# Six weight loads moved behind the first recurrence, and a mixed series of idle products, in a delta-rule attention and feed-forward kernel

## The chip, the cores and the metric

The kernel runs on one core of one Trainium2 chip. The metric is device time in microseconds; a lower time is better. The time before is the median of three runs. A core has five engines with instruction streams of their own: TensorE (PE; its weight loads, PEld, are instructions of their own), VectorE (DVE), ScalarE (ACT), GpSimd (POOL) and SyncE (SP), which here issues nearly all DMA transfers. They meet only at semaphores.

## The reference

Two parts in a row. First a delta rule: for each of 4 x 8 heads a 48 x 48 state is carried over 768 positions.

```python
for t in range(S):
    kt, vt, bt = (k_n[:, :, t], v[:, :, t], beta[:, :, t, None])
    y[:, :, t] = np.einsum('bhd,bhde->bhe', q[:, :, t], state)
    v_old = np.einsum('bhde,bhd->bhe', state, kt)
    state = state + bt[:, :, :, None] * np.einsum('bhd,bhe->bhde', kt, vt - v_old)
```

`k_n` is k over its norm. Then a feed-forward layer over the 3072 tokens, whose 384 columns are the heads' outputs side by side:

```python
h = x @ w_in
g = np.where(pos, h, np.where(neg, 0.0, (h + beta) ** 2 / (4.0 * beta)))
return (g @ w_out).astype(np.float32)
```

with beta = 1, `pos` where h >= 1 and `neg` where h <= -1, and 2048 hidden columns.

## The kernel before, in words

Positions are cut into 12 chunks of 64, and two chunks make a block (the code's G, 0 to 5). Within a chunk the recurrence becomes matrix products and the inverse of a 64 x 64 triangular matrix per head. The inverse is made by DVE for small diagonal blocks (`lanes`, `solve`, `unlanes`) and then put together by PE: `merge16_a` and `merge16_b` join 16-row blocks to 32, `merge32_a` and `merge32_b` join those to 64. `chain_r`, `chain_u`, `chain_y`, `chain_d` carry the state from chunk to chunk; `chain_y` leaves the outputs of a chunk as columns of `xb`, the feed-forward layer's input (part of them by six small DMAs on SP, L386).

The feed-forward layer has 16 weight tiles (`FT`), each with 128 hidden columns of w_in and w_out. They come packed, 768 KB each (`weight_loads`, L83), and are unpacked by a generator (`unpack`, `weight`) in steps on ACT and DVE (L125 to L137) into pairs of float32r parts, a large one and a remainder. `up` makes h (L524), `rest` and the lines around it the activation, `down` adds to the output (L539). A product takes three passes over the pairs of parts.

The order is written out by hand: each engine runs its instructions in the order in which the code issues them, and waits at semaphores.

- SP first issues, in this order, the inputs of chunks 0 and 1 (`load_w(0)`, `load_w(1)`), beta, weight tiles 0 and 1, `load_kv(0)`, `load_kv(1)`, and weight tiles 2 to 15. Transfers on this queue follow each other.
- PE first runs 14 warm-up products (L99), the Gram products of chunks 0 and 1 (`gram`, L146 and L147), and then `hold(KEEP, 512)`: 20 idle products of the zero tile SF, 128 x 128 by 128 x 512 (L473). They use no result and wait for none; DVE meanwhile solves the small blocks. The next work of PE is `merge16_a(0)`, which waits for DVE's transpose (L270).
- Then come the stages of chunk 0 and 1 (L482 to L499). Each `stage` issues PE's products, then steps of the unpacking (`wu`) and the scaling of v (`sv`) on ACT and DVE, then the reading out of the products. After `chain_y(0)` SP issues `load_w(2)`, the inputs of chunk 2 (L72 and L73), and after `chain_d(0)` `load_kv(2)`.
- From L502 on, items (block, weight tile) are run with `plan`, which places the next block's recurrence between them at fixed half items. For block 0 the Gram products of chunks 2 and 3 (L146 again) stand at items 2 and 4, `load_w(3)` at item 1.

PSUM banks for the products of the first part are handed out in rotation by `acc()` from the list START of eight; after `spare.clear()` (L500) the name `ch` with two banks is used. The name `ghi` with two buffers holds the large part of the activation.

In float32 one `nc.tensor.matmul` is two matmul instructions with a weight load each, four PE instructions; in float32r it is one matmul and one weight load.

Of the kernel before, what the change touches and what calls it, by code (L numbers as in the profile page):

```python
# [7 lines left out]
F32 = mybir.dt.float32  # L8
F32R = mybir.dt.float32r
# [4 lines left out]
C = 64  # L14
# [5 lines left out]
DF = 2048  # L20
FT = DF // 128
WARM = 14
KEEP = 20
PASSES = ((0, 0), (0, 1), (1, 0))
WHOLE = 2
LAG = 2
# [3 lines left out]
def delta_rule_moe(ctx: ExitStack, tc: tile.TileContext, kqa, kqb, kv, beta, w, out):  # L30
# [14 lines left out]
    nc = tc.nc  # L45
# [3 lines left out]
    NB = CB * C  # L49
    P = 128  # L50
# [4 lines left out]
    sb = ctx.enter_context(tc.tile_pool(name="sb", bufs=2))  # L55
    ps = ctx.enter_context(tc.tile_pool(name="ps", bufs=1, space=bass.MemoryType.PSUM))
# [6 lines left out]
    def acc():  # L63
        if spare:
            spare.append(spare.pop(0))
            return spare[-1]
        return dict(name="ch", bufs=2)

    def load_w(g, q=nc.sync):
        for i in range(NT):  # L70
            x = W[g, i] = sb.tile([P, 3, NV, C], F32, name="W", bufs=4)
            q.dma_start(out=x[0:C, 0:3:2], in_=kqb[g, i][:, 0:3:2])  # L72
            q.dma_start(out=x[C:C + D, 0:2], in_=kqa[g, i])  # L73

    def load_kv(g, q=nc.sync):
        for i in range(NT):
            KV[g, i] = sb.tile([P, 2, NV, D], F32, name="KV", bufs=4)
            q.dma_start(out=KV[g, i], in_=kv[g, i])

    def weight_loads(n0, n1):  # L80
        for f in range(n0, n1):
            RAW[f] = const.tile([P, 2, 2 * DM], F32, name=f"wt{f}")
            nc.sync.dma_start(out=RAW[f].bitcast(I32), in_=w.bitcast(I32)[:, f])  # L83
# [6 lines left out]
    weight_loads(0, 2)  # L90
    load_kv(0)
    load_kv(1)
    weight_loads(2, FT)

    warm = sb.tile([P, P], F32, name="wx")
    nc.vector.memset(warm, 0.0)
# [14 lines left out]
    SF = const.tile([P, 2 * NU * D + C - D], F32, name="SU")  # L111
# [299 lines left out]
    def finish(evicts):  # L411

        for p in [q() for q in evicts]:
            if p:
                p()

    def products(*pieces):
        return [p() for p in pieces]

    def both(f, g):  # L420
        return [lambda i=i: f(g, i) for i in range(NT)]

    def run(gen, n=99):
        for _ in range(n):
            if next(gen, 0) == 0:
                break
# [28 lines left out]
    def stage(pieces, *fill):  # L455
        evicts = products(*pieces)
        for gen, m in fill:
            run(gen, m)
        finish(evicts)
# [9 lines left out]
    idle = ps.tile([P, 512], F32, **acc())  # L469

    def hold(n, m):
        for _ in range(n):
            nc.tensor.matmul(idle[:, 0:m], SF[:, 0:P], SF[:, 0:m], start=True, stop=True)  # L473
    hold(KEEP, 512)
    run(ln, 2)
    for x in raws:
        x()
# [11 lines left out]
    stage(one_(merge32_b, 1), (sv[1], 2))  # L489
    stage(both(chain_u, 0), (wu, 3))  # L490
    stage(both(chain_y, 0), (wu, 3))
    load_w(2)
    stage(both(chain_d, 0), (wu, 1))
    load_kv(2)
# [21 lines left out]
    def cols(bs):  # L516
        return slice(bs[0] * NB, bs[-1] * NB + NB)
# [132 lines left out]
    for n, item in enumerate(items):  # L650
        H, c = 2 * n, cols(item[2])
# [79 lines left out]
```

## Time and profile before

| | us |
|---|---|
| median of 3 runs | 694.35 (694.16 to 696.31) |
| span of the profiled execution | 693.4 |
| PE busy | 637.4 |
| DVE busy | 437.2 |
| ACT busy | 397.7 |
| POOL busy | 44.8 |
| mean granted clock of PE | 0.956 |

Of the profiled execution the page gives the span, from the first to the last instruction, and no other time. Bytes read from HBM: 33.13 MB; written: 4.72 MB. Rows of the profile name the engine, the line of the kernel, the operation, the output and inputs by the program's names, the shapes and a count. The chain of waits follows the work that ended last back to the start; "issue" in it is time in which the engine waited for nothing that the profile shows. In tables of stretches a row has the busy time of each engine, the clock that was granted to PE as a share of full speed, the mean share of the DMA engines in use, and GB/s.

### The profile page before, as it was taken

Reading aid. Unit: us, or ns where it says so; the run is one execution under the profiler, and the core shown is the slowest. Engines: PE = TensorE matmul, PEld = TensorE weight load, DVE = VectorE, ACT = ScalarE, POOL = GpSimd, SP = SyncE. Lnnn points to the kernel's source line nnn. Section 1 sums busy time; section 2 is a strip of 40 time slices with the busy share of each in tenths; the row PEclk is TensorE's granted clock in tenths of the full one; section 3 lists DMA queues with packets and bytes.
Section 4 is the critical chain, followed back from the end, with each engine's and each line's share of the span. In section 5 each row is a group of like instructions: output and inputs, shape, how many; then the busy total and the mean of one; then the engine's idle time right before and its main releaser. Section 6 shows DMA issues by size and latency. Waiting matters only on the chain.

```text
span 693.4 us, 19365 instructions
## 1 busy us (share of the span) xinstructions
PE 637.4 (92%) x8428; PEld 552.6 (80%) x8428; DVE 437.2 (63%) x920; ACT 397.7 (57%) x720; POOL 44.8 (6%) x90
## 2 busy tenths in 40 slices
PE   9848876899999899999999999999999999999996
PEld 7338765678989788888888888788888788889895
DVE  3848788973455896446896447895457894433332
ACT  4227785556656556644457545557555468556663
POOL 3203042001000200000200000200000200000000
PEclk9956896799999999999999999999999999999999
DMA  8960430000161000043100153100242000001001
GB/s 244 418 267 9 120 103 1 0 3 4 24 171 53 24 1 2 18 109 98 46 2 2 41 122 81 28 1 2 60 123 79 9 1 3 14 12 46 0 1 46
DMA packets 18532, 41.45 MB, mean 60 GB/s; under 512 B 3600, under 2 KB 9104, under 8 KB 18448
## 3 DMA queue, kind: packets, MB, share of 16 engines
q1 hardware_dynamic: 18112, 40.04, 20.0%
q8 instruction: 66, 1.08, 0.7%
q14 instruction: 18, 0.15, 0.1%
q0 software_dynamic: 256, 0.08, 0.1%
q10 hardware_dynamic: 80, 0.10, 0.1%
HBM read 33.13 MB, written 4.72 MB: 55 GB/s over the span
## 4 chain that ended last, share of the span: by engine, by line
PE 54%; DVE 29%; ACT 6%; issue 5%; DMA 2%; SPq 2%; POOL 1%; DVEq 0%; POOLq 0%; ACTq 0%
PE o L539 17%; PE h L524 16%; DVE pr L247 5%; DVE A L249 4%; PE ch L146 4%; DVE glo L643 4%; PE ch L372 3%; DVE s L674 3%; PE ch L352 3%; PE ch L324 2%; PE ch L396 2%; DVE A L204 2%; PE ch L308 2%; DMA W<-in_kqa_dram 2%; PE ch L338 2%
## 5 line engine op out<-in xcount | busy, mean ns | idle before, releaser
L524 PE MATMUL h<-xb,wt 128*128 128x512 f32 (+1 forms) x936 | 230.6, 392 | 11.9 <-DVE s L674 10.6
L524 PEld LDWEIGHTS h<-xb,wt 128*128 128x128 f32 x936 | 166.5, 193 | 50.1 <-DVE s L674 15.8
L539 PE MATMUL o<-wt,ghi 128*128 128x384 f32 x768 | 201.7, 344 | 0.0
L539 PEld LDWEIGHTS o<-wt,ghi 128*128 128x128 f32 x768 | 138.9, 190 | 8.6 <-issue 1.5
L674 DVE TENSOR_TENSOR s<-h,s 128x512 f32<-128x512 f32 (+1 forms) x104 | 67.0, 644 | 112.9 <-ACT s L666 112.5
L539 PE MATMUL o<-wt,glo 128*128 128x384 f32 x384 | 130.9, 341 | 5.8 <-DVE glo L643 5.8
L642 ACT CAST ghi<-s 128x512 fp32r<-128x512 f32 (+1 forms) x104 | 61.3, 589 | 110.4 <-DVE s L674 81.4
L647 ACT ACTIVATE s<-h,half 128x512 f32<-128x512 f32 (+1 forms) x104 | 68.0, 654 | 55.8 <-PE h L524 55.1
L643 DVE TENSOR_TENSOR glo<-s,ghi 128x512 fp32r<-128x512 f32 (+1 forms) x104 | 67.1, 645 | 36.3 <-ACT ghi L642 35.9
L539 PEld LDWEIGHTS o<-wt,glo 128*128 128x128 f32 x384 | 72.8, 190 | 8.0 <-DVE glo L643 8.0
L647 ACT ACTIVATE s<-s,one 128x512 f32<-128x512 f32 (+1 forms) x104 | 71.8, 691 | 2.6
L666 ACT ACTIVATE s<-s 128x512 f32<-128x512 f32 (+1 forms) x104 | 62.3, 599 | 3.3
L146 PE MATMUL ch<-W 48*64 48x128 f32 x336 | 43.1, 278 | 9.3 <-ACT W L155 3.7
L146 PEld LDWEIGHTS ch<-W 48*64 48x64 f32 x336 | 37.2, 136 | 14.9 <-issue 5.5
L147 PE MATMUL ch<-W 48*64 48x128 f32 x336 | 43.4, 279 | 0.0
L247 DVE TENSOR_TENSOR pr<-A 128x30 f32<-128x30 f32 (+14 forms) x120 | 39.4, 328 | 5.5 <-POOL A L218 3.3
L249 DVE TENSOR_TENSOR A<-A,pr 128x30 f32<-128x30 f32 (+14 forms) x120 | 39.8, 332 | 4.4
L163 DVE TENSOR_TENSOR W<-ch,mask 64x256 f32<-64x256 f32 x64 | 27.0, 422 | 18.9 <-ACT GG L150 18.1
L150 ACT COPY GG<-ch 128x256 f32<-128x256 f32 x42 | 15.4, 374 | 38.5 <-PE ch L147 38.5
L147 PEld LDWEIGHTS ch<-W 48*64 48x64 f32 x336 | 37.2, 136 | 0.0
L218 POOL TENSOR_SCALAR_AFFINE_SELECT A<-A 128x1024 f32<-128x1024 f32 x4 | 5.1, 1265 | 365.4 <-DVE A L217 365.4
L407 DVE TENSOR_TENSOR SU<-ch,SU 48x384 f32<-48x384 f32 x40 | 22.2, 555 | 9.2 <-PE ch L396 8.5
(137 smaller groups left out, 705.6 us busy)
## 6 DMA issues: line engine op xcount, KB each, us to landing
wt<-in_w_dram SPq DMA_DIRECT2D x16, 768.0 KB, 13.7
KV<-in_kv_dram SPq DMA_DIRECT2D x24, 384.0 KB, 5.7
W<-in_kqb_dram SPq DMA_DIRECT2D x24, 256.0 KB, 4.7
W<-in_kqa_dram SPq DMA_DIRECT2D x24, 192.0 KB, 4.8
out_dram<-wx SPq DMA_DIRECT2D x47, 96.0 KB, 2.2
xb<-X SPq DMA_DIRECT2D x66, 32.0 KB, 2.0
xb<-A SPq DMA_DIRECT2D x6, 32.0 KB, 2.0
beta_sb<-in_beta_dram POOLq DMA_DIRECT2D x8, 10.0 KB, 2.4
```

What stands on the lines that cost most here:

```text
L146: nc.tensor.matmul(gp[0:C, p], w_[C:C + D, 0, u, :], w_[C:C + D, 0:2, u, :], start=True, stop=True)
L147: nc.tensor.matmul(gp[C:P, p], w_[0:D, 0, u, :], w_[0:D, 0:3:2, u, :], start=True, stop=True)
L163: nc.vector.tensor_tensor(out=w_[r:r + C, s, us[0]:us[0] + NP], in0=gp[r:r + C, :, 1, :], in1=mask[r:r + C, None, :].broadcast_to([C, NP, ...
L247: nc.vector.tensor_tensor(out=pr, in0=A[:, 0:n, j:j + 1].broadcast_to([P, n, m]), in1=A[:, j:j + 1, j + 1:32].broadcast_to([P, n, m]), op= ...
L249: nc.vector.tensor_tensor(out=A[:, 0:n, j + 1:32], in0=A[:, 0:n, j + 1:32], in1=pr, op=ALU.add)
L524: nc.tensor.matmul(h[:, cols(bs)], WT[f][:, 0, x, k * P:(k + 1) * P], XB[G][:, y, k, cols(bs)], start=(n == 0), stop=(n == 8))
L539: nc.tensor.matmul(oacc[G, k], (ghi, glo)[x][:, k * P:(k + 1) * P], WT[f][:, 1, y, :], start=(new and n == 0), stop=(left[G, b] == 0 and n ...
L642: nc.scalar.copy(out=ghi[:, c], in_=s[:, c])
L643: nc.vector.tensor_tensor(out=glo[:, c], in0=s[:, c], in1=ghi[:, c], op=ALU.subtract)
L647: nc.scalar.activation(out=out, in_=in_, func=AF.Relu, bias=bias, scale=scale)
L666: nc.scalar.activation(out=s[:, c], in_=s[:, c], func=AF.Square)
L674: nc.vector.tensor_tensor(out=s[:, c], in0=h[:, c], in1=s[:, c], op=ALU.max)
```

## The change

Weight tiles 2 to 9 stay where they were; the loads of tiles 10 to 15 are issued after the stage of `chain_y(0)`, before `load_w(2)`. The 20 idle products become 12 of the same form, then 32 and 16 products of zeros of 64 x 64 by 64 x 64 over the four quarters of the array in two orders, 6 products of a float32r tile of zeros (128 x 128 by 128 x 512), 32 products of 32 x 32 by 32 x 32 on four blocks of the array, and 4 of the first form. They write to `idle` and to a second PSUM bank, `other`, taken from the rotation. The zeros in float32r are written by POOL into a buffer of the name `ghi`.

```diff
-KEEP = 20
+KEEP = 12
+SOON = 10
...
-    weight_loads(2, FT)
+    weight_loads(2, SOON)
...
     hold(KEEP, 512)
+    other = ps.tile([P, 512], F32, **acc())
+    zr = sb.tile([P, 2 * NB], F32R, name="ghi", bufs=2)
+    nc.gpsimd.memset(zr.bitcast(F32), 0.0)
+
+    def quarters(n, w, order):
+        for j in range(n):
+            for r, c in order:
+                nc.tensor.matmul((idle, other)[r // C][c:c + w, j * w:j * w + w], SF[r:r + w, 0:w], SF[r:r + w, 0:w], start=True, stop=True)
+    quarters(8, C, ((0, 0), (C, C), (C, 0), (0, C)))
+    quarters(4, C, ((0, 0), (0, C), (C, 0), (C, C)))
+    for _ in range(6):
+        nc.tensor.matmul(idle, zr[:, 0:P], zr, start=True, stop=True)
+    for j in range(8):
+        for r, c in ((32, 0), (96, C), (0, 32), (C, 96)):
+            nc.tensor.matmul((idle, other)[r // C][c:c + 32, j * 32:j * 32 + 32], SF[r:r + 32, 0:32], SF[r:r + 32, 0:32], start=True, stop=True)
+    hold(4, 512)
     run(ln, 2)
...
     stage(both(chain_y, 0), (wu, 3))
+    weight_loads(SOON, FT)
     load_w(2)
```

## The prediction

> **What bounds the kernel now.** I read the page first, then the chain of waits, then the engine timelines of the first 100 us, where every edit lies.
>
> ```profile
> span 693.4 us, 19365 instructions
> PE 637.4 (92%) x8428; PEld 552.6 (80%) x8428; DVE 437.2 (63%) x920; ACT 397.7 (57%) x720; POOL 44.8 (6%) x90
> q8 instruction: 66, 1.08, 0.7%
> ```
>
> Over the span PE is the bound, but the edits lie in the first recurrence, between 34 and 65 us, and there it is another. The chain, in order of time (start, length, what):
>
> ```profile
> 32.09 2.19 DVE XT L270
> ...
> 36.42 4.21 issue
> ...
> 42.54 4.17 issue
> ...
> 48.60 1.83 issue
> ...
> 52.60 1.29 issue
> 53.88 2.82 PE o L308 x97
> ...
> 57.42 0.46 issue
> ```
>
> These five stretches of "issue" are 4.21 + 4.17 + 1.83 + 1.29 + 0.46 = 11.96 us in which PE waits for no engine and no tile. The PE timeline says what they are:
>
> ```profile
> 34.42 1.63 PE L281 MATMUL ch<-XT,GG 32*32 32x16 f32 x127 [2.76 <-DVE XT L270]
> 35.83 0.21 PE L281 MATMUL h<-XT,GG 32*32 32x16 f32 x1
> 35.87 0.21 PE L281 MATMUL ch<-XT,GG 32*32 32x16 f32 x1
> 35.87 0.55 PE L281 MATMUL h<-XT,GG 32*32 32x16 f32 x25
> 40.63 1.53 PE L281 MATMUL h<-XT,GG 32*32 32x16 f32 x100 [4.21 <-issue]
> 41.95 0.24 PE L293 MATMUL h<-A,XT 32*32 32x16 f32 x2
> 41.99 0.22 PE L281 MATMUL h<-XT,GG 32*32 32x16 f32 x2
> 42.01 0.53 PE L293 MATMUL h<-A,XT 32*32 32x16 f32 x24
> ```
>
> Between the first two stalls PE runs 100 + 2 + 2 + 24 = 128 matmuls, with their 128 weight loads 256 instructions. The queue q8 moved 66 packets, and PE's 2 x 8428 instructions over 66 are 255 each: q8 is PE's instruction fetch, and PE stops at the end of a block of 256 until the next has come. Before the first stall it ran 154 pairs, 308 instructions: 52 of one block and the whole next. So one block is fetched ahead, asked for when PE enters the block before. From entry to the next block's arrival: 40.63 to 46.70, **6.07 us**; then 46.70 to 50.43, 50.43 to 53.88, 53.88 to 57.89 (the ends of the stalls), mean **3.73 us**. What changes in between is the data transfers, in a table of stretches:
>
> ```profile
> 26.00:28.00 2.00, 2.00 (x6) 0.86 (x5) 1.79 (x7) 0.00 (x0) 0.00 (x0) 1.00 1.00 412
> 44.00:46.00 2.00, 0.00 (x0) 0.00 (x0) 0.00 (x0) 0.15 (x1) 0.00 (x0) 0.50 0.83 331
> 64.00:66.00 2.00, 2.00 (x50) 2.00 (x48) 0.68 (x2) 1.47 (x4) 0.00 (x0) 0.60 0.01 4
> ```
>
> (Columns: busy PE, PEld, DVE, ACT, POOL; granted clock, DMA share, GB/s.) The sixteen weight tiles fill the DMA engines until 0.83 of the way through 44 to 46, about 45.6 us. A fetch costs 6.07 us under them and 3.73 us without. A merge of 16-row blocks has 256 instructions, one block, and runs in 1.9 us (40.63 to 42.54): even a free DMA leaves this stage bound by the fetch.
>
> **The change, part by part.**
>
> *Six weight loads leave the front.* One is 768 KB, at 412 GB/s 1.91 us; six are 11.45 us, so the DMA engines come free at 45.6 - 11.45 = 34.1 us instead of 45.6.
>
> *The idle products.* One 128x512 product is two matmuls and two weight loads. Their time, and nearest rows for the other forms (the PE timeline and, for L352, L524 and L308, the chain):
>
> ```profile
> 14.22 17.43 PE L473 MATMUL ch<-SU 128*128 128x512 f32 x40
> 149.74 1.26 PE L281 MATMUL ch<-XT,GG 32*32 32x16 f32 x128 [0.21 <-DVE KV L343]
> 176.62 2.00 PE ch L352 x64
> 154.49 2.29 PE h L524 x9
> 167.40 1.13 PE ch L308 x64
> ```
>
> Twenty took 17.43 us (0.87 each). The new series: 12 big ones 10.46 us. Then 48 products on 64x64 quarters, 96 matmuls: the 64x64 matmuls of L352 go at 31 ns on two quarters, on all four between 31 and half of it, so 1.5 to 3.0 us. Six float32r products: L524 has that form, 0.254 us each, 1.5 us. Then 32 products of 32x32, 64 matmuls, between the 9.8 ns of L281 on four blocks and the 17.7 ns of L308 on two: 0.6 to 1.1 us. Four big ones 3.49 us. Sum 17.6 to 19.6 us; it ends between 31.8 and 33.8, before DVE has the transpose (34.28) on which the merge waits. I take 33.4. The PE gap before the merge shrinks from 2.76 us to about 1; a shorter gap alone gains nothing, because DVE sets the start.
>
> *Their instructions.* Before: 20 x 4 = 80. After: 48 + 128 + 64 + 12 + 128 + 16 = 396, 316 more. The merge began with 308 instructions in hand; 308 - 316 + 256 = **248** now, with the following block asked for 8 instructions, two big products, before the idle series ends: 33.4 - 1.7 = 31.7 us. That block's predecessor is asked for in the first quarters, near 26, and with 6.07 us arrives near 32, so I take 32.0: a stall inside the series of well under 1 us, which the 0.9 us before 34.28 cover.
>
> *The fetches, one after another.* Asked at 32.0, the first missing block comes between 32.0 + 3.73 = 35.7 and 32.0 + 6.07 = 38.1; the DMA engines come free in the middle, so I take 36.9. The following come every 3.73 us: 40.6, 44.4, 48.1, 51.8. They open instruction 248, 504, 760, 1016, 1272 of the stage; before, 308, 564, 820, 1076, 1332 opened at 40.63, 46.70, 50.43, 53.88, 57.89. The 60 instructions from 1272 to 1332 are 30 pairs of L308, 2.82 us for 97, 0.87 us: 52.7 against 57.89, **PE gains 5.2 us**. The second merge step of group 0 ends at instruction 768, just past 760, near 44.7.
>
> *What is late next.* DVE and ACT, which unpack the weights between the merges:
>
> ```profile
> 48.36 0.42 DVE L298 TENSOR_TENSOR XT<-XT,h 128x256 f32<-128x256 f32 x1 [8.54 <-PE h L293]
> ...
> 63.25 0.96 DVE L131 SCALAR_TENSOR_TENSOR xb<-wt,xb 128x768 int32<-128x768 int32 x1
> ...
> 66.35 0.96 DVE L137 TENSOR_TENSOR wt<-xb,wt 128x768 fp32r<-128x768 f32 x1 [1.67 <-ACT wt L135]
> ...
> 65.49 0.83 ACT L135 CAST wt<-xb 128x768 fp32r<-128x768 f32 x1
> ```
>
> From L298 at 48.36 DVE works with almost no gap until 64.68 (66.35 less its idle 1.67), so it gains what the second merge gains: 48.36 - 44.7 = 3.7 us. ACT's L135 at 65.49 needs L131, done at 64.21, 1.28 us earlier: it may gain 3.7 + 1.28 = 4.9. The smaller of 5.2 and 4.9 goes on: **-4.9 us** at the outputs of the first chunk.
>
> *The six loads in their new place* stand on SP's queue behind L386 and ahead of the second block's inputs, load_w(2) and load_kv(2); their 11.45 us of data go first.
>
> ```profile
> 2.00:4.00 2.00, 2.00 (x11) 2.00 (x11) 1.24 (x1) 0.30 (x2) 1.00 (x1) 1.00 0.85 210
> 73.39 1.40 SPq L72 DMA_DIRECT2D W<-in_kqb_dram  x1
> 74.83 0.59 SPq L73 DMA_DIRECT2D W<-in_kqa_dram  x1
> W<-in_kqa_dram SPq DMA_DIRECT2D x24, 192.0 KB, 4.8
> xb<-X SPq DMA_DIRECT2D x66, 32.0 KB, 2.0
> 87.12 0.29 PE L146 MATMUL ch<-W 48*64 48x128 f32 x1 [2.53 <-issue]
> 88.32 0.29 PE L146 MATMUL ch<-W 48*64 48x128 f32 x1
> 90.09 0.92 ACT L125 ACTIVATE xb<-wt 128x768 f32<-128x768 f32 x1
> 90.88 0.65 ACT L150 COPY GG<-ch 128x256 f32<-128x256 f32 x2
> ```
>
> All in the clock of before. The first tile starts moving near 73.4 + 1.8 (the small transfers land after 2.0), six end at 86.7, the first half of W(2), 448 KB at the 210 GB/s of such rows, at 88.8. The other bound: it landed at 74.83 + 4.8 = 79.6, plus 11.45 is 91.1. Its reader, the Gram product, began at 87.12; ACT takes the first result at 90.88, though it was done 1.2 us after the start: 2.6 us of cover. So 1.7 to 4.0 us late, less 2.6: 0 to 1.4 us, I take **+0.7**. Queued behind a waiting Gram product are PE's next products, behind a waiting L150 ACT's whole queue. Their own readers are no concern: tile 10 is first read by the eleventh L125, at 90.09. The issue of W(3), KV and the staging rows moves back as well, but their readers come later than W(2)'s by more than that.
>
> *At no cost:* the memset of the float32r operand and the second PSUM bank.
>
> ```profile
> 18.39 3.80 POOL L156 TENSOR_SCALAR_AFFINE_SELECT W<-W 64x256 f32<-64x256 f32 x8 [5.31 <-ACT W L155]
> ```
>
> POOL idles 5.31 us before its next work, and a memset of this size is half a us; without that gap it would delay L156 by as much. Every later bank of the rotation moves on by one, to banks emptied as long ago as before.
>
> **Sum.** 693.4 - 4.9 + 0.7 = 689.2 us of span. Of the profiled execution the page shows only the span, 0.95 us below the median of the runs, 694.35; so **690.2 us**.
>
> The Trainium skill, "Runtime: NRT & Kernel Launch", section "Instruction fetch mechanics", has blocks of 256 instructions as here, but says the fetch is hidden because issue is slower than the fill. By it the stalls would not be fetches and the time would stay near 694; the row above (256 instructions, then 4.17 us) speaks against it. It is the last rival below.
>
> **The rivals.**
>
> *More than I say (687.5).* If the first block comes by the free price, 35.7, and the rest at the best interval, 3.45: instruction 1332 at 35.7 + 4 x 3.45 + 0.87 = 50.4, 7.5 us gained on PE; the second merge at 42.9, 5.5 on DVE, 6.8 through ACT; nothing lost on W(2). For it: the queue is empty 2 us after the request. Against: the one fetch seen at the end of the transfers, asked for at 40.63, took the full 6.07.
>
> *The small products count as idle (692.9).* In the rows above the granted clock is 0.50 while 32x32 merges fill PE. If the quarters let it fall near 28 us, the rest of the series runs at half: it has reached 28 after 1.0 of the 1.5 us of float32r, the other 0.5 takes 1.0, the 32x32 products 1.7, the four big ones 7.0, end 37.7. The merge starts 3.3 us late but with its blocks in hand: instruction 248 at 39.6, the next ones at 43.3, 47.1, 50.8, 54.5, so 1332 at 55.4, 2.5 us gained on PE; the second merge at 47.4, 1.0 on DVE, 2.2 through ACT, less 0.7. Against: dense 64x64 products brought the clock back between 64 and 66 us.
>
> *Slower (699.4): the second block's inputs are starved.* The six tiles may move at the 210 GB/s of the mixed load instead of 412: 22.5 us, W(2) at 99.8, 12.7 us late less 2.6: +10.1 - 4.9. It outweighs the gain as soon as W(2) lands after 87.1 + 2.6 + 4.9 = 94.6. For it: rows of W are in that mix, and stand right behind the tiles. Against: tiles alone moved at 412 GB/s.
>
> *It doesn't do what it says (694.3).* The fetch is slow for another reason than the tiles, and stays at 6 us; the longer idle series then only moves the block borders.
>
> **How the numbers follow.** Forecast 0.56, more 0.17, counted as idle 0.11, starved 0.11, nothing 0.05. A measurement of this kernel tells 0.3%, 2.1 us, from no change: faster is below 692.3, slower above 696.4. Faster: 0.17, and 0.52 of the forecast's 0.56 and 0.02 from the idle case, 0.71. Slower: 0.11 and 0.01. Same: the rest, 0.17. The forecast's own range is 687.9 to 692.8 (the first block by its ends, W(2) by its own); the range of 8 in 10 takes in the first rival and the idle one: 686.3 to 695.0.
>
> **What would show it.** Right: "issue" before 60 us falls from 12 to about 6 us; the DMA share falls under 0.2 near 34; the first stall stands some 124 pairs into the merges and ends near 37; L298 starts near 44.7, L135 (now 65.49) near 60.6. Wrong: a stall still of 4 us at the second block; the merge starting after 34.6; a clock of 0.50 before 34; PE L146 of the second block waiting on DMA for more than 3 us.

## The result: 698.12 us, slower, and the profile after

The changed kernel takes 698.12 us (median of 18 runs, 695.31 to 702.79); the kernel before took 694.68 beside it (18 runs, 692.12 to 696.72). The ratio is 1.0052, 95% interval 1.0036 to 1.0069: slower by half a per cent. Forecast were 690.2 us, range 686.3 to 695.0. The profiled execution after took 697.55, with this on its page (span; PE's row; the queue of instruction fetches):

```profile
span 695.8 us, 19683 instructions
PE 637.3 (92%) x8586; PEld 554.8 (80%) x8586; DVE 437.6 (63%) x920; ACT 397.8 (57%) x720; POOL 45.3 (7%) x91
q8 instruction: 67, 1.10, 0.7%
```

PE's busy time is that of before (637.4): the 2.4 us are waiting. Lines of the changed kernel stand one further than before up to the idle products, and 17 or 18 further behind them: L281 is L282, L72 is L73, L146 is L147, L524 is L542.

**Up to 65 us the forecast came about.** The PE timeline after (start, length, line, operation, tiles, shapes, count, and in brackets the idle time before it with what ended it):

```profile
13.93 10.57 PE L474 MATMUL ch<-SU 128*128 128x512 f32 x24
24.42 1.63 PE L483 MATMUL ch<-SU 64*64 64x64 f32 x96
25.98 1.65 PE L487 MATMUL ch<-ghi 128*128 128x512 f32 x6
27.57 0.75 PE L490 MATMUL ch<-SU 32*32 32x32 f32 x64
...
30.81 1.88 PE L474 MATMUL ch<-SU 128*128 128x512 f32 x4 [0.58 <-issue]
34.15 1.22 PE L282 MATMUL h<-XT,GG 32*32 32x16 f32 x124 [1.46 <-DVE XT L271]
37.58 1.91 PE L282 MATMUL h<-XT,GG 32*32 32x16 f32 x128 [2.21 <-issue]
41.30 0.29 PE L282 MATMUL h<-XT,GG 32*32 32x16 f32 x4 [1.82 <-issue]
45.13 1.90 PE L294 MATMUL o<-A,XT 32*32 32x16 f32 x128 [1.85 <-issue]
48.86 0.24 PE L294 MATMUL o<-A,XT 32*32 32x16 f32 x3 [1.83 <-issue]
52.58 0.26 PE L309 MATMUL o<-XT,GG 32*32 32x32 f32 x2 [0.20 <-issue]
56.30 0.37 PE L325 MATMUL ch<-GG 32*32 32x32 f32 x5 [0.19 <-issue]
```

The series ends at 32.69 and the merge still starts when DVE lets it. The stalls of the merges sum to 2.21 + 1.82 + 1.85 + 1.83 + 0.20 + 0.19 = 8.10 us where five stretches of 11.96 stood. The table of stretches shows the DMA engines free just before 34:

```profile
32.00:34.00 2.00, 0.69 (x2) 0.00 (x0) 2.00 (x2) 0.00 (x0) 0.00 (x0) 1.00 0.82 336
34.00:36.00 2.00, 1.22 (x124) 1.15 (x124) 1.97 (x4) 0.00 (x0) 0.00 (x0) 1.00 0.11 42
```

The timelines of DVE and ACT after carry the gain on (the line set apart is the kernel before):

```profile
45.47 0.42 DVE L299 TENSOR_TENSOR XT<-XT,o 128x256 f32<-128x256 f32 x1 [5.92 <-PE o L294]
58.85 0.97 ACT L357 COPY SU<-h 64x384 f32<-64x384 f32 x2
61.29 0.83 ACT L136 CAST wt<-xb 128x768 fp32r<-128x768 f32 x1
```

```profile
63.04 0.97 ACT L356 COPY SU<-ch 64x384 f32<-64x384 f32 x2
```

The addition after the second merge is 48.36 - 45.47 = 2.9 us earlier, ACT's cast 65.49 - 61.29 = 4.2, and the first read-out of chunk 0 (L356 before, L357 after) 63.04 - 58.85 = 4.2.

**Behind 69 us it is lost.** The chain of waits after, which now runs through SP's queue (start, length, what):

```profile
69.12 1.34 SPq L84
...
72.72 0.46 SPq L84
...
73.98 15.49 DMA W<-in_kqa_dram
...
89.61 0.44 PE ch L147
```

The PE and ACT timelines at that place, and the stretches (three after, then one before):

```profile
78.85 1.32 PE L542 MATMUL h<-xb,wt 128*128 128x256 f32 x9
89.61 0.44 PE L147 MATMUL ch<-W 48*64 48x128 f32 x1 [9.43 <-DMA W<-in_kqa_dram]
...
91.62 0.37 ACT L151 COPY GG<-ch 128x256 f32<-128x256 f32 x1 [5.00 <-PE ch L148]
93.33 0.37 ACT L151 COPY GG<-ch 128x256 f32<-128x256 f32 x1 [1.33 <-PE ch L148]
```

```profile
80.00:84.00 4.00, 0.17 (x2) 0.00 (x0) 3.91 (x8) 1.95 (x4) 0.00 (x0) 1.00 1.02 375
84.00:88.00 4.00, 0.00 (x0) 0.00 (x0) 3.97 (x7) 1.57 (x3) 0.00 (x0) 0.57 1.06 200
88.00:92.00 4.00, 2.39 (x23) 2.42 (x25) 0.50 (x1) 0.37 (x1) 0.00 (x0) 0.50 0.71 201
```

```profile
88.00:94.00 6.00, 4.31 (x58) 3.61 (x54) 5.11 (x9) 4.46 (x12) 1.88 (x4) 1.00 0.97 252
```

PE stands still for 9.43 us because the first half of W(2) comes only at 89.47 (73.98 + 15.49). The Gram product of chunk 2, 4.2 us early until then, begins 2.5 us late (89.61 for 87.12), and at half the clock that it had before. The rest of the span keeps this: DVE's transpose of the next block's small matrices (L204, now L205) starts at 115.20, before at 113.36, and the span ends 2.4 us later.

### The profile page after: what moved, and what is told of

The parts are those of the page before. It is cut to its first block, busy times and chain, and to the rows that moved or that the text cites. A ratio compares the mean times of both kernels' runs of the same rounds, so it can differ in the third digit from the quotient of the medians.

```text
span 695.8 us, 19683 instructions
## 1 busy us (share of the span) xinstructions
PE 637.3 (92%) x8586; PEld 554.8 (80%) x8586; DVE 437.6 (63%) x920; ACT 397.8 (57%) x720; POOL 45.3 (7%) x91
## 4 chain that ended last, share of the span: by engine, by line
PE 56%; DVE 29%; ACT 5%; issue 4%; DMA 3%; SPq 1%; POOL 1%; DVEq 0%; POOLq 0%; ACTq 0%
PE o L557 18%; PE h L542 16%; PE ch L147 5%; DVE pr L248 5%; DVE A L250 4%; DVE glo L661 4%; DVE s L692 3%; PE ch L373 3%; PE ch L353 2%; DMA W<-in_kqa_dram 2%; PE ch L325 2%; PE ch L397 2%; PE ch L309 2%; DVE A L205 2%; PE ch L339 1%
## 5 line engine op out<-in xcount | busy, mean ns | idle before, releaser
L542 PE MATMUL h<-xb,wt 128*128 128x512 f32 (+1 forms) x936 | 228.9, 390 | 14.1 <-DVE s L692 12.6
L542 PEld LDWEIGHTS h<-xb,wt 128*128 128x128 f32 x936 | 165.3, 192 | 51.6 <-DVE s L692 17.7
L147 PE MATMUL ch<-W 48*64 48x128 f32 x336 | 43.2, 279 | 13.4 <-DMA W<-in_kqa_dram 9.4
L147 PEld LDWEIGHTS ch<-W 48*64 48x64 f32 x336 | 37.5, 137 | 18.8 <-issue 12.4
```

The costliest lines, as they stand in the source:

```text
L147: nc.tensor.matmul(gp[0:C, p], w_[C:C + D, 0, u, :], w_[C:C + D, 0:2, u, :], start=True, stop=True)
L542: nc.tensor.matmul(h[:, cols(bs)], WT[f][:, 0, x, k * P:(k + 1) * P], XB[G][:, y, k, cols(bs)], start=(n == 0), stop=(n == 8))
```

## The experiments

The theory (Q where a letter stands for it): the moved loads alone bring the gain in the first recurrence, by shorter fetches, and the same loads spend it again, because the second block's inputs stand behind them on SP's queue. Its rivals: the new series makes the difference, by the borders of the instruction blocks or by a cost of its own; or the gain is lost for a reason that has nothing to do with the order on the queue.

All ratios are against the kernel before, run beside on the same chip. "Read-out" is the first read-out of chunk 0, "Gram" the first Gram product of chunk 2, both from each kernel's one profiled execution; executions of one kernel differ by some 2 us, so the ratios decide.

| kernel | idle series | tiles 10 to 15 stand | ratio (95%) | read-out | Gram |
|---|---|---|---|---|---|
| before | 20 large | in front | 1 | 63.04 | 87.12 |
| after | new | ahead of W(2) | 1.0052 (1.0036 to 1.0069) | 58.85 | 89.61 |
| e1 | new | in front | 1.0025 (1.0009 to 1.0042) | 63.61 | 85.57 |
| e2 | 20 large | ahead of W(2) | 1.0014 (0.9998 to 1.0030) | 58.15 | 88.89 |
| e3 | new | behind KV(2) | 0.9978 (0.9963 to 0.9992) | 59.17 | 82.81 |
| e4 | 20 large | behind KV(2) | 0.9949 (0.9933 to 0.9964) | 58.07 | 82.32 |
| e5 | small ones first | behind KV(2) | 1.0056 (1.0029 to 1.0082) | 60.20 | 82.34 |
| e6 | new | 3 ahead of W(2), 3 behind KV(2) | 0.9976 (0.9957 to 0.9996) | 59.51 | 84.20 |
| e7 | small ones first | 2 behind KV(2), 4 behind KV(3) | 1.0011 (0.9996 to 1.0026) | 59.71 | 81.82 |
| e8 | 20 large | 2 behind KV(2), 4 behind KV(3) | **0.9898 (0.9879 to 0.9917)** | 57.38 | 79.65 |
| e9 | small ones first, 12 more | behind KV(2) | 0.9991 (0.9968 to 1.0015) | 59.12 | 83.06 |
| e10 | 20 large, 15 small | in front | 0.9974 (0.9959 to 0.9990) | 64.23 | 88.08 |
| e11 | 20 large, 15 small | behind KV(2) | 0.9954 (0.9934 to 0.9974) | 60.11 | 82.44 |
| e12 | new | 2 behind KV(2), 4 behind KV(3) | 0.9943 (0.9923 to 0.9962) | 59.57 | 83.29 |
| e13 | new without float32r | behind KV(2) | 0.9968 (0.9949 to 0.9987) | 57.72 | 79.66 |
| e14 | new without small products | behind KV(2) | 0.9942 (0.9923 to 0.9962) | 58.03 | 80.14 |
| e15 | 20 large, one in the second bank | behind KV(2) | 0.9929 (0.9912 to 0.9945) | 57.66 | 81.68 |

### One part of the change alone (e1, e2)

Only the new series, all sixteen tiles in front (against the changed kernel):

```diff
-    weight_loads(2, SOON)
+    weight_loads(2, FT)
...
-    weight_loads(SOON, FT)
```

> The new idle series alone; all sixteen weight tiles stay in front. Theory Q (the moved loads bring the gain and, standing ahead of W(2), the loss; the series does next to nothing): the fetches still cost about 6 us until the tiles have landed near 45.6, so the first read-out of chunk 0 (ACT L357, at 63.0 before and 58.9 in the changed kernel) comes at 61.5 to 63, no wait on the DMA of W(2), time 693 to 694.7. Rival S (the series brings the gain): L357 near 59 and a time near 690. Rival E (the loss comes from what the series changes, the bank rotation or the block borders): slower than before, 697 or more.

Only the loads, with the old series (against the kernel before):

```diff
-    weight_loads(2, FT)
+    weight_loads(2, 10)
     ...
     stage(both(chain_y, 0), (wu, 3))
+    weight_loads(10, FT)
     load_w(2)
```

> The old series of 20 idle products, with the six loads ahead of W(2) as in the changed kernel. Q: the first recurrence ends as early as in the changed kernel (first read-out of chunk 0 at 58 to 60 us), PE then waits 8 to 10 us on the DMA of W(2), time 697 to 699. S: the first recurrence stays as before (read-out near 63) and the wait costs as much, 700 or more. E: no loss, 690.

The PE timeline with the new series alone:

```profile
34.00 1.22 PE L282 MATMUL h<-XT,GG 32*32 32x16 f32 x124 [1.27 <-DVE XT L271]
40.17 1.90 PE L282 MATMUL h<-XT,GG 32*32 32x16 f32 x128 [4.95 <-issue]
46.36 0.29 PE L282 MATMUL h<-XT,GG 32*32 32x16 f32 x4 [4.29 <-issue]
```

and with the loads alone, at the same place and at chunk 2:

```profile
38.19 1.52 PE L281 MATMUL h<-XT,GG 32*32 32x16 f32 x100 [1.94 <-issue]
41.80 1.52 PE L293 MATMUL h<-A,XT 32*32 32x16 f32 x99 [1.71 <-issue]
...
88.89 0.44 PE L146 MATMUL ch<-W 48*64 48x128 f32 x1 [10.62 <-DMA W<-in_kqa_dram]
```

The gain of the first recurrence belongs to the loads alone: without them the stalls stay at 4.95 and 4.29 us and the read-out at 63.61, with them it comes at 58.15 under the old series too. So does the loss: 10.62 us of waiting for W(2). The series brings nothing at the merges, and its kernel is 0.25% slower than before. Both kernels miss the times that theory Q gave them, e1 on the slow side and e2 on the fast one; what the series costs is taken up below.

### Where the loads stand (e3, e4, e6)

The changed kernel with the six loads behind `load_kv(2)` (e3); e4 is the same with the old series:

```diff
-    weight_loads(SOON, FT)
     load_w(2)
     stage(both(chain_d, 0), (wu, 1))
     load_kv(2)
+    weight_loads(SOON, FT)
```

> The changed kernel with the six loads issued after load_kv(2) instead of before load_w(2). Q: the first recurrence as in the changed kernel, no wait of PE on W(2); the second chunk's Gram product near 82.7 instead of 89.6; W(3) behind the tiles may come up to 2 us late; time 690 to 692. S and E: the place of the loads is not the cause, 697 to 699.

> The old series of 20 idle products and the six loads after load_kv(2): the kernel before with nothing changed but the place of six loads. Q: within 1 us of the run with the new series and this place, 690 to 692. S: no gain in the first recurrence, 694 to 695.

And three tiles at either place (e6):

```diff
-    weight_loads(SOON, FT)
+    weight_loads(SOON, 13)
     load_w(2)
     stage(both(chain_d, 0), (wu, 1))
     load_kv(2)
+    weight_loads(13, FT)
```

> The changed kernel with three of the six tiles ahead of load_w(2) and three behind load_kv(2). A tile takes 1.9 us of the queue, so the wait of PE on the DMA of W(2), 9.4 us with six, falls to 3 to 4 us and the time to 694 to 695.5. If what delays W(2) is the one ring that falls behind and not the amount of data, the wait stays above 6 us.

The Gram product of chunk 2 with the loads behind KV(2), from its PE timeline:

```profile
82.81 0.29 PE L147 MATMUL ch<-W 48*64 48x128 f32 x1 [2.53 <-issue]
```

and with three tiles ahead:

```profile
84.20 0.44 PE L147 MATMUL ch<-W 48*64 48x128 f32 x1 [5.00 <-DMA W<-in_kqa_dram]
```

Behind KV(2) nothing waits for W(2): PE's 2.53 us there are the ones before had too, and the product starts 87.12 - 82.81 = 4.3 us early. The order on the queue alone is worth 1.0052 - 0.9978 = 0.74% with the new series and 1.0014 - 0.9949 = 0.65% with the old, some 5 us. With three tiles the wait is 5.00 us, with six 9.43. The ratio of e6 equals e3's within its interval, so three tiles ahead cost little; its profiled execution (698.04) lies 5.3 us above its median (692.76), and the clock of that stretch differs, so the three and the six are compared by the waits only.

### Behind the second block's inputs as well (e7, e8, e12)

Six loads behind KV(2) in their turn stand ahead of W(3). So two tiles there, and the other four after `load_kv(3)`, here with the old series (e8, against e4):

```diff
     load_kv(2)
-    weight_loads(10, FT)
+    weight_loads(10, 12)
...
+            at(fill, G, 2, (weight_loads, (12, FT)))
```

> The old series of 20 products, tiles 10 and 11 behind load_kv(2), 12 to 15 behind load_kv(3). Beside the run with the old series and all six behind load_kv(2) (0.9949 of before): up to 2 us less if W(3) was late there, else the same within 0.7 us.

> The changed kernel's series, tiles 10 and 11 behind load_kv(2), 12 to 15 behind load_kv(3). With the old series this split took 0.9949 to 0.9898. If tiles 12 to 15 delayed W(3) and the staging rows there, the same step here: 0.992 to 0.994 of before, W(3) landing before 88 us instead of 94. If the two results differ for another reason, 0.998.

SP's timeline with all six behind KV(2) (e4), and with the split (e8):

```profile
72.73 3.50 SPq L83 DMA_DIRECT2D wt<-in_w_dram  x6
77.26 9.89 SPq L386 DMA_DIRECT2D xb<-A  x6
88.52 0.64 SPq L72 DMA_DIRECT2D W<-in_kqb_dram  x1
```

```profile
72.01 0.91 SPq L83 DMA_DIRECT2D wt<-in_w_dram  x2
74.59 4.51 SPq L386 DMA_DIRECT2D xb<-A  x6
79.94 0.64 SPq L72 DMA_DIRECT2D W<-in_kqb_dram  x1
...
86.04 3.13 SPq L83 DMA_DIRECT2D wt<-in_w_dram  x4
```

W(3) is issued at 79.94 in place of 88.52: the six small loads in front of it take 4.51 us in place of 9.89, behind two tiles and not six. The ratio falls by 0.51% with the old series and 0.35% with the new one (e12 to e3). e8, 688.36 us, is faster than both kernels: 1.0% under the one before, and its interval (0.9879 to 0.9917) lies wholly under e4's.

That W(3)'s earlier issue is what brings this is not shown. In e4 nothing waits for W(3): its first half is in at 94.66, and the Gram product of chunk 3 starts at 95.81 without a gap. And of the 2.9 us by which e8's profiled span is shorter (688.9 and 686.0), 82.32 - 79.65 = 2.7 are there at the Gram product of chunk 2, ahead of W(3)'s reader; over 70 to 76 us the granted clock was 0.64 in e4 and 1.00 in e8. A wait for W(3) does stand in the trace of e5 (below), 3.70 us, and none in e7, the same series with the split, which is 0.45% faster.

### When the next block of instructions is asked for (e5, e9)

The prediction had the merges' first missing block asked for when PE enters the block before it. Both kernels put the small products ahead of the large ones, so that this entry lies long before the merges. e5, against e3 (the series begins with the quarters, and ends with 44 products of 32x32 in place of 32 and 14 large ones in place of four):

```diff
-    hold(KEEP, 512)
...
-    for j in range(8):
+    for j in range(11):
...
-    hold(4, 512)
+    hold(14, 512)
```

> The six loads behind load_kv(2); an idle series with its small products first (48 of the quarters, 6 float32r, 44 of 32x32) and then 14 big ones, 47 instructions longer than the changed kernel's. It asks for the block at instruction 961 some ten us before the merges instead of 3, so that these begin with about 466 instructions in hand, where the run with the changed kernel's series has 250 and waits 2.48 us for the next block. If the block borders set the pace of the first recurrence, the first stall in the merges comes after some 230 pairs, the read-out of chunk 0 (59.2 there) near 56.5, and the time is 2 to 2.5 us below that run's. If DVE and ACT set it, the read-out stays within 0.7 us and the time too.

e9 has twelve more small products, so that 94 instructions of the block ahead of the missing one, not 47, are behind PE when it waits for DVE:

```diff
-    for j in range(11):
+    for j in range(14):
```

> The run with the small products first began its merges 46 instructions past a block border and yet had asked for no further block: the fetch started 1.0 us after the merges did. Here 48 more instructions of small products, 94 past the border when PE comes to the merge's wait. If the request goes out some 50 to 90 instructions after the border, the fetch starts inside the idle series (22 to 33 us), the merges begin with 162 + 256 = 418 instructions in hand and stall first after 209 pairs. If it goes out later than that, the first stall stands after 81 pairs and the fetch starts 1 us after the merges. No claim on the time beyond 1 us.

e7 is e5's series with e8's order of loads.

> The series with the small products first, tiles 10 and 11 behind load_kv(2), tiles 12 to 15 behind load_kv(3). If the six tiles also delay chunk 3 (W(3) landed at 94.2 where its Gram products began at 95.8 with the old series), up to 2 us below the run with all six behind load_kv(2); if W(3) was in time, the same within 0.7 us.

The PE timeline of e5, at the merges and, after the dots, in the second block:

```profile
22.83 10.46 PE L474 MATMUL ch<-SU 128*128 128x512 f32 x24 [1.13 <-issue]
34.79 1.05 PE L282 MATMUL h<-XT,GG 32*32 32x16 f32 x104 [1.50 <-DVE XT L271]
38.68 1.90 PE L282 MATMUL h<-XT,GG 32*32 32x16 f32 x128 [2.84 <-issue]
...
97.42 0.29 PE L147 MATMUL ch<-W 48*64 48x128 f32 x1 [3.70 <-DMA W<-in_kqa_dram]
160.03 0.45 PE L556 MATMUL o<-wt,ghi 128*128 128x384 f32 x1 [0.88 <-issue]
164.03 0.29 PE L294 MATMUL ch<-A,XT 32*32 32x16 f32 x2 [2.21 <-issue]
```

and of e9:

```profile
22.27 0.38 PE L489 MATMUL ch<-SU 32*32 32x32 f32 x20 [2.73 <-issue]
22.58 13.98 PE L474 MATMUL ch<-SU 128*128 128x512 f32 x28
36.49 1.95 PE L282 MATMUL h<-XT,GG 32*32 32x16 f32 x208
40.42 0.71 PE L282 MATMUL h<-XT,GG 32*32 32x16 f32 x48 [1.98 <-issue]
```

In e5 PE entered the block at 22.83 and stood 47 instructions into it at the wait; the trace's DMA records have the fetch of the missing block starting at 35.77, 0.98 us after the merge began. In e9 the fetch started at 25.90, inside the series, about 50 instructions into the block, and the merges ran 208 pairs before their first stall in place of 104. So the request goes out some 50 instructions behind the border: later than 47 by e5, and by about 50 at the latest by e9. A PE that waits less than that far into a block asks for nothing while it waits. In the changed kernel the border lay 8 instructions ahead of the wait, and the fetch started at 35.17, 1.02 us after the merge. Neither kernel gained by it. In e9 the series itself stalled (0.95 and 2.73 us), ended late, and the merge began at 36.49. e5 was expected 2 to 2.5 us below e3 and is 0.78% above it. Its trace shows losses late: the wait of 3.70 us for W(3), and two stalls at block borders in the second block's merges, 0.88 and 2.21 us, where e3 has one of 0.28. e7 has these two as well (0.61 and 1.94). Where the borders fall can cost time in a later stage of small products too.

### What the new series costs (e10, e11, e13, e14, e15)

At equal places of the loads the new series is slower each time: 1.0052 to 1.0014, 1.0025 to 1, 0.9978 to 0.9949, 0.9943 to 0.9898, that is 0.25 to 0.45%, 2 to 3 us. First the borders of the blocks, moved by 60 instructions with the old series (e10, against before; e11 the same against e4):

```diff
     hold(KEEP, 512)
+    for j in range(15):
+        nc.tensor.matmul(idle[0:32, j * 32:j * 32 + 32], SF[0:32, 0:32], SF[0:32, 0:32], start=True, stop=True)
```

> The kernel before, all loads in front, with 15 idle products of 32x32 (60 instructions, about 0.3 us, under the wait for DVE) after the 20: the block borders stand where the changed kernel's series puts them (316 is 256 + 60), without its float32r, its quarters and its second bank. If the borders are what the series costs, it behaves as the run with the new series alone: first stall of the merges after some 124 pairs, 0.25% slower than before (0.1 to 0.4%). If another part of the series costs it, within 0.1% of before, and the merges' first stall is no dearer than 4.2 us.

> The old series with all six loads behind load_kv(2) (0.9949 of before), and the same 15 small products. Borders: as the run with the new series and this place (0.9978): read-out of chunk 0 about 1 us later than with the old borders, time 0.998 of before. Another part of the series: 0.995.

Both put the first stall after 124 pairs, as the new series does, and neither is slower (0.9974 to 1, 0.9954 to 0.9949): the borders aren't it. e10, which differs from the kernel before by 15 idle products alone, is even 0.26% faster, and no run shows why. So a single difference of this size doesn't prove a cost; what speaks for one is that all four pairs have the same sign. Then the series without its float32r products (e13, against e3), without all products on parts of the array (e14, against e3), and the second bank alone (e15, against e4):

```diff
-    for _ in range(6):
-        nc.tensor.matmul(idle, zr[:, 0:P], zr, start=True, stop=True)
+    hold(2, 512)
```

> The late loads behind KV(2) with the new series, its six float32r products put back as two 128x512 products (1.74 us for 1.65). Known: the new series here 0.9978, the old series 0.9949 of the kernel before. If the float32r products cost the 0.3% (for example by a change of mode, or by a lower load that the clock answers): 0.995. If the 64x64 and 32x32 products cost it: 0.998, unchanged.

```diff
-    quarters(8, C, ((0, 0), (C, C), (C, 0), (0, C)))
-    quarters(4, C, ((0, 0), (0, C), (C, 0), (C, C)))
+    hold(2, 512)
...
-    for j in range(8):
-        for r, c in ((32, 0), (96, C), (0, 32), (C, 96)):
-            ...
+    hold(1, 512)
```

> The late loads behind KV(2) with a series of 12 large products, 2 and 1 large ones in place of the 48 quarter products and the 32 small ones, 6 float32r products, 4 large ones: 316 instructions fewer less 12 more, and no product on less than the whole array. If the small products cost the 0.3% (by their instructions or by the clock): 0.995, and the stream stalls by no issue inside the series. If the float32r products or the second bank cost it: 0.998.

```diff
-    hold(KEEP, 512)
+    hold(KEEP - 1, 512)
+    other = ps.tile([P, 512], F32, **acc())
+    zr = sb.tile([P, 2 * NB], F32R, name="ghi", bufs=2)
+    nc.gpsimd.memset(zr.bitcast(F32), 0.0)
+    nc.tensor.matmul(other, SF[:, 0:P], SF[:, 0:512], start=True, stop=True)
```

> The late loads behind KV(2) with the old series of twenty, one of which writes the second accumulator, so that each later tile of the rotation stands one bank further, and the float32r operand cleared but not used. If the shifted rotation costs the 0.3%: 0.998, against 0.9949 with one bank. If the products do: 0.995.

The second bank, the shifted rotation and the memset show no cost (0.9929, e4 0.9949). With the float32r products but no small ones the cost is gone (0.9942, e3 0.9978); with the small ones but no float32r most of it is there (0.9968, whose interval lies above e15's, though it overlaps e14's and e4's). That points to the 80 small products, and is not firm. How 2 to 3 us would reach the end is not shown: the merge starts at much the same time (e3 34.46, e4 34.09), and while the read-outs of the four kernels with moved loads and the whole new series (after, e3, e6, e12) lie at 58.85 to 59.57 and those without small products at 57.38 to 58.15, e13 with them has 57.72 and e11, with fifteen and no cost, 60.11.

## Why the prediction was wrong

**The fetches and the gain: right, a little smaller.** The stages' stalls were blocks of 256 instructions under a DMA load, and the load's end set their length: shown by e2 against before, and by the changed kernel against e1, which differ in the loads alone. DMA free at 34.1, measured just under 34; first stall after 124 pairs, measured 124; its end 36.9, measured 37.58, inside 35.7 to 38.1; the following blocks 3.73 apart, measured 3.72, 3.83 and 3.73. Stalls of about 6 us forecast, 8.10 measured. The second merge's addition 44.7, measured 45.47; ACT's cast 60.6, measured 61.29; the gain 4.9, measured 4.2 (with the old series, e2, 63.04 - 58.15 = 4.9). The rival in which the transfers don't matter has fallen, and so has the smaller-gain rival (a clock of 0.50 before 34): the clock stood at 1.00 until 36. The row from which that rival took its clock, 44 to 46, has no PE product in it at all. By the Trainium skill, "Runtime: NRT & Kernel Launch", section "Instruction fetch mechanics", the fetch should be mostly hidden; the trace disagrees, since moving six transfers alone (e2) took the first two stalls from 4.21 and 4.17 to 1.94 and 1.71 us.

**A sub-step failed without harm.** "Asked for when PE enters the block before" is wrong: the request comes some 50 instructions later (e5, e9). The block that was to be asked for at 32.0 started to move at 35.17, and PE went on 37.58 - 35.17 = 2.41 us later; the forecast had 3.73 to 6.07 from the request on. Two errors of opposite sign gave a first block 0.7 us late: that it came so near is luck.

**The step that failed: "I take +0.7" for the six loads in their new place.** Compared with e3, where W(2) stands ahead of the tiles, it measured +6.4 in the profiled executions (worked out below) and 0.74%, 5.1 us, by the ratios; and every piece of it was short. In the clock of before the first half of W(2) was to land at 88.8 to 91.1; it landed at 89.47 + 4.2 = 93.7, 4.9 behind the lower end. The first tile, forecast to move from 75.2 - 4.2 = 71.0 and to be in at 72.9, was in at 74.33 (1.4 us). From there five more at 1.88 us, the interval of the first three (74.33, 76.19, 78.08), would have ended at 83.7; the sixth landed at 87.20 (3.5 us). Of the sixteen parts into which the transfer is split, fifteen of the sixth tile had landed by 84.09: one of the sixteen lagged, by 0.1 us at the third tile, 1.5 at the fourth and 3.1 at the sixth. Of W(2)'s first half fifteen parts were in at 86.67 and the last at 89.47, when PE went on. The rate of a stretch, 412 GB/s, says nothing of that one part, and a transfer has landed when its last part has. The lag is there in e2 as well (sixth tile: fifteen parts by 84.05, the last at 86.91). The first half of W(2) took 2.27 us after the tiles, as forecast (2.1).

Then the cover. W(2)'s reader started 6.7 us later than the gain would have let it (89.61 + 4.2 - 87.12, to rounding). ACT's cover of 2.6 us was there, but the Gram products ran at half the clock (0.50 from 84.57 to 94.81 in the trace's clock records; 1.00 in this place before): the first result was taken 91.62 - 89.61 = 2.0 us after the start, and the second 1.33 us of waiting later. Compared with e3, where nothing waits, ACT's second read-out ends 93.70 - 87.31 = 6.4 us later, and the span is 695.8 - 689.9 = 5.9 us longer. The sum of the profiled executions closes: 693.4 - 4.2 + 6.4 = 695.6, measured 695.8.

**The rival that was nearest.** "Starved" named the place, the mechanism and the sign: W(2) late, PE waiting over 3 us. Its breakeven was W(2) in after 94.6; it came at 93.7. So with the old series the lateness and the half clock took the gain and no more than 0.14% on top (e2, 1.0014, whose interval takes in 1); the rest of the loss is the series'. Its price was for another reason than the one that occurred: the tiles moved at 396 to 427 GB/s between 72 and 80, not at 210.

**"At no cost" failed for the small products.** The second bank and the memset did cost nothing (e15). The mixed series costs 2 to 3 us; e13 and e14 point to its small products, and by which path is open. In the profiled execution this isn't a term of its own, since single executions differ by as much. By the ratios it is the second step that failed, a term put at nothing: the moved loads alone, with nothing late, bring 0.51% (e4, 3.5 us); their place ahead of W(2) takes 0.65% (e2, 4.5 us); the series takes 0.38% (the changed kernel against e2, 2.6 us). That adds up to 0.52% slower, where the forecast had 4.9 us of gain, 0.7 of loss and nothing for the series.

**What remains open.** Why one part of sixteen lags: its first step, at the fourth tile, falls near one of PE's own instruction fetches (78.75, one packet of 1.06 us), which is argued from the times, not shown. And whether the half clock follows from PE's idle 9.43 us: e3, with no long wait, also shows 0.72 over 82 to 88. By which path the split of the loads (e8) gains, and why e10 is faster than before, is open too.

## What to carry to other kernels

A transfer that is moved to free a busy stretch is paid for by whatever stands behind it on its queue: put it behind the inputs that are read next, and try that for each of the blocks that follow (here, with the old series, 1.0014 ahead of W(2), 0.9949 behind KV(2), 0.9898 with four of the six behind KV(3)). Price the delay by when the last part of the transfer lands and not by the mean rate, and don't count a cover that was measured at a full clock. That a series of idle products ends before the wait doesn't make it free; try it alone.

## What the runs showed of the hardware that wasn't expected

- The next block of 256 PE instructions is asked for some 50 instructions into a block: with 47 behind it at a wait PE asked after the wait, with 94 during the series (e5, e9).
- In a row of 768 KB transfers one of sixteen parts fell 3.1 us behind the others, and the reader of the transfer behind them waited for its last part (89.47, fifteen in at 86.67).
- The granted clock can be at half while large products run. In e9 small products and two stalls (0.95 and 2.73 us) come first; which of the two counts isn't shown. Large products start at 22.58, and the stretches have

```profile
22.00:24.00 2.00, 1.73 (x23) 1.03 (x23) 1.73 (x8) 0.96 (x2) 1.35 (x2) 0.90 1.04 427
24.00:26.00 2.00, 2.00 (x3) 0.67 (x2) 1.79 (x7) 0.00 (x0) 0.00 (x0) 0.50 1.03 417
```

- 64x64 matmuls in turn over four quarters of the array went at 1.63 us / 96 = 17 ns each, against 31 ns for those of L352 (48 columns) on two quarters.
